# Other places for the steps of a spectral slot, and the spectrum's sum in PSUM

## Chip, cores and metric

One core of a Trainium2 chip runs the program. The metric is the device time of one execution in microseconds, as the median of several runs.

## What is computed

```python
X = np.fft.rfft(x, axis=1)                      # x: 8 x 3008 x 256
Yr = Xr @ w_r - Xi @ w_i + b_r
Yi = Xr @ w_i + Xi @ w_r + b_i
Yr, Yi = [np.sign(Y) * np.maximum(np.abs(Y) - 0.01, 0) for Y in (Yr, Yi)]
y = np.fft.irfft(Yr + 1j * Yi, n=3008, axis=1)
t = y.reshape(24064, 256)
g = t @ w_gate                                  # 256 x 1536
out = (g / (1 + np.exp(-g)) * (t @ w_val)) @ w_out
```

## The kernel before

The program has two parts: a **spectral part** (Fourier transform, mixing, shrinking, inverse transform), some 600 us long, and the feed-forward part (FFN), which takes the rest. In the FFN every product is cut into 2 x 2 blocks that take seven block products in place of eight (a Strassen scheme), and an operand is a pair of tiles, a rounded upper part and the rest (`hi`, `lo`), so that a product is three matmuls. The spectral part ends in DRAM (`xt_d`), and the FFN reads its tokens from there.

The spectral part is a pipeline of 96 **slots** (8 batches x 12). `transform` does not issue a step at once: `put(t, step)` records it with a time in slots, and `go` sorts all records by that time and issues them. So the numbers set the order on each engine, and each engine works through its own queue in that order and waits on semaphores. The steps of slot s are, with TensorE as PE, VectorE as DVE, ScalarE as ACT, GpSimd as POOL and the DMA queue as SP:

- `load_a` (L360, SP) and `b_mm` (L365, PE): 4 fp32 matmuls, the second stage of the transform, into bank `ps_b`.
- `f_steps` (L378): `im` (ACT) copies the imaginary part out of PSUM, `hi` (ACT) rounds the bank to `f_hi`; on DVE, `both` (L388) adds the real and imaginary part into the tile `f`, `hi_sum` (L394) rounds that sum, `lo_sum` (L397) takes its rest, `lo` (L400) takes the rest of the bank.
- `sum_mm` (L404, PE): six matmuls of the rounded sum and its rest into half a bank, `ps_s`. `add_bias` (L411, DVE) adds the bias and writes the result into a `mixb` bank; `mix_mm` (L417, PE) adds twelve more matmuls onto it.
- `y_steps` (L433): `turn` (ACT, four copies, L439), `clip` (DVE, L443), `shrink` (POOL, L446), `upper` (ACT, `y_hi`, L452), `lower` (DVE, `y_lo`, L455).
- `bi_mm` (L459, PE), `z_out` (L470, ACT), `z_store` (L475, SP), three to four slots later.

Between these stand **items**, none to four in a slot: `a_mm` (L344), the first stage of the transform for later batches, and `ai_mm` (L490), the last stage of the inverse. Each is followed by a copy on ACT (`a_out`, L350; `ai_out`, L496) and a store. `GAPS` gives an item's place in its slot, `AFTER` that of its copy. `A_FAST`, `A_SLOW`, `Z_AT`, `Z_SLOW` and `Z_FAST` say in which slots the items fall.

Eighteen **weight units** run beside that (L264): a load, eight DVE steps that turn float64 weights into float32 (L280 to L287), four sums on POOL (`sums`, L291), a rounding on ACT (`upper`, L303), a subtraction on POOL (`lower`, L308), a store. At the end `open_ring` (L620) frees space for a ring of four buffers, `load_unit` (L624) fills it, and the FFN's first products (L670) are issued among the last steps of the spectral part by `run` (L912).

Of the kernel before, what the change touches and what calls it, by code (L numbers as in the profile page):

```python
# [9 lines left out]
F32 = mybir.dt.float32  # L10
# [3 lines left out]
ALU = mybir.AluOpType  # L14
# [15 lines left out]
T = 512  # L30
# [6 lines left out]
HIDDEN = [P, 6, T]  # L37

KEPT = 6
A_FAST, A_KNEE, A_SLOW = 2.0, 36, 1.35  # L40
FIRST_X = {2: -0.93, 3: -0.90, 4: -0.5}
W_FIRST, W_STEP = 2, 4.2
A_SUM = False
WARM = 5
LAG, LAST = 4, 2.2
PAD = 216
Z_AT, Z_SLOW, Z_KNEE, Z_FAST = 18, 2.8, 19, 1.1
NG, GT, GW = 13, 5 * N1, 6 * N1
NU = 7
WO = 12 * GW + 4 * N1  # L50
GAPS = {1: (0.38,), 2: (0.38, 0.78), 3: (0.38, 0.78, 0.90), 4: (0.38, 0.40, 0.78, 0.90), 5: (0.36, 0.38, 0.40, 0.78, 0.90)}
AFTER = {0.36: 0.62, 0.38: 0.63, 0.40: 0.64, 0.78: 1.03, 0.90: 1.15}


A_AT = {1: 0, 2: 1, 4: 2, 5: 3, 6: 4, 7: 5, 3: 6}
# [127 lines left out]
def transform(ctx, tc, front, last, tail, ffn, ps_, xp, w_r, w_i, cb, wup_raw, wdn_raw, ca, cf, ci, co, wdn, w21, wup_d, xt_d, d2):  # L183
# [24 lines left out]
    def put(t, fn, *args):  # L208
        ops.append((t, len(ops), fn, args))
# [12 lines left out]
    d1, st = {}, {}  # L222
# [41 lines left out]
    def weight_unit(i, at):  # L264
        kind, u = ("up", i) if i < 2 * NQ else ("down", i - 2 * NQ)
        src = wup_raw[u] if kind == "up" else wdn_raw[u]
        e = scratch[:, 2 * T : 3 * T].bitcast(I32)
        w = scratch[:, : 2 * T].rearrange("p (a b) -> p a b", b=P)
        a = w[:, 0:4, :].rearrange("p a b -> p (a b)")
        m = w[:, 4:8, :].rearrange("p a b -> p (a b)")  # L270
        box = {}
        high = lambda: box["raw"][:, :, 1]
        low = lambda: box["raw"][:, :, 0]

        def load():
# [13 lines left out]
        a21, a11, a12, a22, s1, s2, s3, s4 = [w[:, j, :] for j in range(8)]  # L289

        def sums():  # L291
            g.tensor_tensor(s1, a21, a22, op=ALU.add)
            g.tensor_tensor(s2, s1, a11, op=ALU.subtract)
            g.tensor_tensor(s3, a11, a21, op=ALU.subtract)
            g.tensor_tensor(s4, a12, s2, op=ALU.subtract)

        def upper():
            if kind == "up":
                box["both"] = sb.tile([P, 2, 7, P], F32R, name="both", tag="both", bufs=1)
                box["hi"], box["lo"] = box["both"][:, 0], box["both"][:, 1]  # L300
            else:
                box["hi"], box["lo"] = [part[:, u] for part in wdn]
            act.copy(box["hi"], w[:, 1:8, :])  # L303
            if i == 3 * NQ - 1:
                act.copy(w21[:, 0, :], a21)

        def lower():
            g.tensor_tensor(box["lo"], w[:, 1:8, :], f32(box["hi"]), op=ALU.subtract)  # L308
            if i == 3 * NQ - 1:
                g.tensor_tensor(w21[:, 1, :], a21, f32(w21[:, 0, :]), op=ALU.subtract)  # L310

        def store():
            if kind == "up":
                nc.sync.dma_start(wup_d[u], f32(box["both"].rearrange("p i n a -> p i (n a)")))

        put(at - 1.5, load)
        for step, t in zip(steps, (0.39, 0.93, 0.96, 1.39, 1.93, 1.96, 2.39, 2.93)):
            put(at + t, step)
        put(at + 3.36, sums)
        put(at + 3.72, upper)  # L320
        put(at + 4.36, lower)
        put(at + 4.8, store)


    def load_first():
# [49 lines left out]
    def f_steps(b, p):  # L375
        box = {}

        def im():  # L378
            box["bank"] = st.pop(("b", b, p)).rearrange("p (a q b) -> p q a b", q=2, b=64)
            f = sb.tile([P, 2, C], F32, name="f", tag="f", bufs=2)  # L380
            box["im"], box["both"] = f[:, 0, :], f[:, 1, :]
            box["hi"] = sb.tile([P, 3, 2, P], F32R, name="f_hi", tag="f_hi", bufs=2)
            box["lo"] = sb.tile([P, 3, 2, P], F32R, name="f_lo", tag="f_lo", bufs=2)
            st["f", b, p] = box["hi"], box["lo"]
            act.copy(split(box["im"]), box["bank"][:, 1:2])

# [45 lines left out]
    def y_steps(b, p):  # L432
# [175 lines left out]
class FFN:  # L608
# [51 lines left out]
    def run(self, go, one):  # L660
# [347 lines left out]
```

## Time and profile before

| | us |
|---|---|
| median of 3 runs (2651.88 to 2654.41) | 2652.49 |
| the profiled execution's own time | 2655.08 |
| its span, first to last instruction | 2653.0 |
| spectral part, from the first sums on (38 to 598 us of the span) | 560.0 |
| FFN after it (598 to 2653) | 2055.0 |
| PE busy over the span | 2618.5 (99%) |
| DVE, ACT, POOL busy | 2079.8, 1739.5, 1919.7 |

PE counts as busy while any matmul is in flight, and a matmul's end is modelled. A short wait between two products can so hide in the busy time, and the share of 99% says little: the starts of the matmuls say more. The profiled execution took 2.6 us more than the median.

### The profile page before, as it was taken

Reading aid. Unit: us, or ns where it says so; the run is one execution under the profiler, and the core shown is the slowest. Engines: PE = TensorE matmul, PEld = TensorE weight load, DVE = VectorE, ACT = ScalarE, POOL = GpSimd, SP = SyncE. Lnnn points to the kernel's source line nnn. Section 1 sums busy time; section 2 is a strip of 40 time slices with the busy share of each in tenths; the row PEclk is TensorE's granted clock in tenths of the full one; section 3 lists DMA queues with packets and bytes.
Section 4 is the critical chain, followed back from the end, with each engine's and each line's share of the span. In section 5 each row is a group of like instructions: output and inputs, shape, how many; then the busy total and the mean of one; then the engine's idle time right before and its main releaser. Section 6 shows DMA issues by size and latency. Waiting matters only on the chain.

```text
span 2653.0 us, 39572 instructions
## 1 busy us (share of the span) xinstructions
PE 2618.5 (99%) x12984; PEld 2190.5 (83%) x12984; DVE 2079.8 (78%) x3101; ACT 1739.5 (66%) x3356; POOL 1919.7 (72%) x1459
## 2 busy tenths in 40 slices
PE   8999999999999999999999999999999999999999
PEld 5787878897888888888888888888888888888899
DVE  4888888666877787778777787878778887888787
ACT  5787877686666666666666666566666666666665
POOL 1343343247888888888888888888888888888886
PEclk8999999999999999999999999999999999999999
DMA  9999987884544554445544554454444444444453
GB/s 270 304 300 300 299 274 244 261 274 143 168 159 156 172 176 157 163 156 174 166 160 152 177 170 160 157 175 160 145 141 167 157 146 144 163 157 154 153 174 126
DMA packets 191033, 494.71 MB, mean 186 GB/s; under 512 B 17989, under 2 KB 99317, under 8 KB 190709
## 3 DMA queue, kind: packets, MB, share of 16 engines
q1 hardware_dynamic: 190829, 492.18, 56.9%
q8 instruction: 104, 1.70, 0.3%
q14 instruction: 100, 0.82, 0.1%
HBM read 381.49 MB, written 110.62 MB: 185 GB/s over the span
## 4 chain that ended last, share of the span: by engine, by line
PE 91%; DVE 4%; ACT 2%; DMA 2%; issue 1%; POOL 0%; SPq 0%; DVEq 0%; ACTq 0%; POOLq 0%
PE bank L670 76%; PE mixb L423 3%; PE ps_a L348 2%; PE ps_b L370 2%; PE ps_x L156 2%; PE ps_s L409 2%; PE ps_z L468 2%; DVE f_hi L394 1%; PE bank L156 1%; ACT t L439 1%; DMA d<-a 1%; DVE f L388 1%; DVE scratch L283 0%; DMA xt_d<-xt 0%; ACT f_hi L391 0%
## 5 line engine op out<-in xcount | busy, mean ns | idle before, releaser
L670 PE MATMUL bank<-x_parts,wup 128*128 128x512 f32 (+1 forms) x6048 | 1511.0, 385 | 0.3 <-DVE bank L805 0.2
L670 PEld LDWEIGHTS bank<-x_parts,wup 128*128 128x128 f32 x6048 | 1127.9, 188 | 221.8 <-DVE bank L805 2.8
L690 POOL TENSOR_TENSOR h_parts<-more,h_parts 128x512 fp32r<-128x512 f32 (+1 forms) x572 | 847.5, 1494 | 109.6 <-ACT h_parts L686 108.9
L690 POOL TENSOR_TENSOR h_parts<-hidden,h_parts 128x512 fp32r<-128x512 f32 (+1 forms) x431 | 562.4, 1315 | 208.0 <-ACT h_parts L686 187.8
L670 PE MATMUL bank<-h_parts,wdn_hi 128*128 128x512 f32 (+1 forms) x2014 | 612.2, 385 | 0.0
L686 ACT CAST h_parts<-hidden 128x512 fp32r<-128x512 f32 (+1 forms) x433 | 265.6, 614 | 454.7 <-DVE hidden L778 454.7
L778 DVE TENSOR_TENSOR hidden<-hidden,bank 128x512 f32<-128x512 f32 (+1 forms) x576 | 375.9, 674 | 78.2 <-PE bank L670 69.5
L670 PEld LDWEIGHTS bank<-h_parts,wdn_hi 128*128 128x128 f32 x2014 | 377.0, 188 | 72.0 <-POOL h_parts L690 0.5
L711 DVE TENSOR_TENSOR sums<-sums,bank 128x512 f32<-128x512 f32 (+1 forms) x357 | 240.3, 673 | 250.0 <-PE bank L670 249.9
L446 POOL TENSOR_TENSOR t<-t,y 128x512 f32<-128x512 f32 x96 | 122.5, 1276 | 385.8 <-DVE y L443 365.7
L670 PE MATMUL bank<-h_parts,wdn_lo 128*128 128x512 f32 (+1 forms) x1007 | 390.1, 387 | 0.0
L686 ACT CAST h_parts<-more 128x512 fp32r<-128x512 f32 (+1 forms) x572 | 349.7, 611 | 35.1 <-DVE more L681 24.3
L776 ACT ACTIVATE hidden<-bank 128x512 f32<-128x512 f32 (+1 forms) x432 | 252.6, 585 | 120.0 <-PE bank L670 115.6
L681 DVE TENSOR_TENSOR more<-hidden 128x512 f32<-128x512 f32 (+1 forms) x286 | 289.7, 1051 | 0.0
L681 DVE TENSOR_TENSOR more<-hidden,more 128x512 f32<-128x512 f32 (+1 forms) x286 | 256.5, 897 | 0.0
L783 ACT COPY bank<-bank 128x512 f32<-128x512 f32 (+1 forms) x288 | 161.6, 561 | 110.8 <-DVE hidden L778 103.7
L805 DVE TENSOR_TENSOR bank<-hidden,bank 128x512 f32<-128x512 f32 (+1 forms) x288 | 197.0, 684 | 39.2 <-PE bank L670 23.9
L658 POOL TENSOR_TENSOR x_parts<-xf,x_parts 128x512 fp32r<-128x512 f32 (+1 forms) x168 | 210.8, 1273 | 18.7 <-ACT x_parts L657 14.6
L670 PEld LDWEIGHTS bank<-h_parts,wdn_lo 128*128 128x128 f32 x1007 | 189.0, 188 | 35.1 <-DVE sums L711 0.2
L791 ACT COPY hidden<-bank 128x512 f32<-128x512 f32 (+1 forms) x288 | 167.6, 582 | 2.9 <-PE bank L670 0.5
L439 ACT COPY t<-mixb 64x256 f32<-64x256 f32 x384 | 141.0, 367 | 19.7 <-PE mixb L423 15.8
L828 DVE TENSOR_TENSOR hidden<-hidden,bank 128x512 f32<-128x512 f32 (+1 forms) x144 | 97.4, 676 | 43.7 <-PE bank L670 42.7
(104 smaller groups left out, 3055.2 us busy)
## 6 DMA issues: line engine op xcount, KB each, us to landing
wup<-wup_d SPq DMA_DIRECT2D x288, 896.0 KB
d<-a SPq DMA_DIRECT2D x128, 192.0 KB
a_in<-d SPq DMA_DIRECT2D x96, 256.0 KB
d<-z SPq DMA_DIRECT2D x96, 256.0 KB
out<-o SPq DMA_DIRECT2D x88, 256.0 KB
scratch<-xp SPq DMA_DIRECT2D x116, 192.0 KB
xt_d<-xt SPq DMA_DIRECT2D x36, 470.0 KB
xf<-xt_d SPq DMA_DIRECT2D x15, 1024.0 KB
```

The costliest lines, as they stand in the source:

```text
L439: act.copy(t[64 * half : 64 * half + 64, k * C : (k + 1) * C], mixed[p % 2][64 * k : 64 * k + 64, half * C : (half + 1) * C])
L658: self.tc.nc.gpsimd.tensor_tensor(part[:, 1, :h], src, f32(part[:, 0, :h]), op=ALU.subtract)
L670: nc.tensor.matmul(o, lhsT=weights[w], rhs=parts[x], start=start and i == 0, stop=stop and i == 2, skip_group_check=True)
L681: v.tensor_tensor(at(o, h), at(a, h), at(b, h), op=ALU.subtract)
L686: act.copy(pair[i][:, 0, :h], at(i, h))
L690: eng.tensor_tensor(pair[i][:, 1, :h], at(i, h), f32(pair[i][:, 0, :h]), op=ALU.subtract)
L711: v.tensor_tensor(o, o, spare[:, :h], op=ALU.add)
L776: act.activation(at(i, h), src, AF.Silu)
L778: v.tensor_tensor(at(i, h), at(i, h), src, op=ALU.mult)
L783: act.copy(b3[:, :h], b1[:, :h])
L791: act.copy(m5, b2[:, :h])
L805: v.tensor_tensor(b2[:, :h], m5, b3[:, :h], op=ALU.add)
```

## The change

The tables of places get other numbers, every step's; many steps had their places written at the call and now take them from tables at the head. The spectrum's sum (`both`) is written into the free half of the bank `ps_s` (in the diff `SUM_PSUM`) in place of the tile `f`; that bank is so taken at `both`, no longer at `sum_mm`. `SHRINK` and `A_SUM` are off: `shrink` stays on POOL. The work itself is the same, instruction for instruction.

```diff
-A_FAST, A_KNEE, A_SLOW = 2.0, 36, 1.35
-W_FIRST, W_STEP = 2, 4.2
-Z_AT, Z_SLOW, Z_KNEE, Z_FAST = 18, 2.8, 19, 1.1
-GAPS = {1: (0.38,), 2: (0.38, 0.78), 3: (0.38, 0.78, 0.90), 4: (0.38, 0.40, 0.78, 0.90), 5: (0.36, 0.38, 0.40, 0.78, 0.90)}
-AFTER = {0.36: 0.62, 0.38: 0.63, 0.40: 0.64, 0.78: 1.03, 0.90: 1.15}
+A_FAST, A_KNEE, A_SLOW = 2.0, 36, 1.378
+Z_AT, Z_SLOW, Z_KNEE, Z_FAST = 19.318, 2.802, 19, 1.013
+W_FIRST, W_STEP, W_LOAD = 2, 4.249, 1.492
+W_AT = (0.188, 0.8711, 1.2132, 1.4363, 1.8494, 1.8495, 2.2706, 2.9687)
+W_LATE = (2.971, 3.565, 3.797, 4.6)
+SUM_PSUM, SHRINK, A_SUM = True, False, False
+B_AT = 0.381
+F_AT = (0.394, 0.511, 0.443, 0.604, 0.625, 0.699)
+S_AT = (1.074, 1.184, 1.443)
+Y_AT = (1.003, 1.045, 1.046, 1.785, 1.888)
+I_AT = (-0.074, 0.086, 0.813)
+AHEAD = (1.796, 1.84, 1.768)
+STORE = (0.313, 0.176)
+X_AT = (85.19, 2.457, 86.085, 1.851)
+GO_FIRST, GO = 0.225, (0.082, 0.896, 1.085, 1.221, 1.555, 2.104)
+GAPS = {1: (0.399,), 2: (0.399, 0.4923), 3: (0.399, 0.4923, 0.9754), 4: (0.399, 0.4272, 0.4923, 0.9754), 5: (-0.2439, 0.399, 0.4272, 0.4923, 0.9754)}
+AFTER = {-0.2439: -0.021, 0.399: 0.449, 0.4272: 0.899, 0.4923: 1.056, 0.9754: 1.057}
...
-        for step, t in zip(steps, (0.39, 0.93, 0.96, 1.39, 1.93, 1.96, 2.39, 2.93)):
-        put(at + 3.36, sums)
-        put(at + 3.72, upper)
-        put(at + 4.36, lower)
+        for step, t in zip(steps, W_AT):
+        put(at + W_LATE[0], sums)
+        put(at + W_LATE[1], upper)
+        put(at + W_LATE[2], lower)
...
         def both():
+            st["s", b, p] = ps_.tile([P, T], F32, name="ps_s")
+            box["both"] = st["s", b, p][:, C:] if SUM_PSUM else box["sum"]
             v.tensor_tensor(split(box["both"]), box["bank"][:, 0:1], split(box["im"]), op=ALU.add)
...
-        put(s + 0.23, b_mm, b, p)
-        for fn, t in zip(f_steps(b, p), (0.40, 0.60, 0.41, 0.66, 0.71, 0.78)):
-        put(s + 1.0, sum_mm, b, p)
-        put(s + 1.26, add_bias, b, p)
-        put(s + 1.53, mix_mm, b, p)
-        for fn, t in zip(y_steps(b, p), (0.80, 1.05, 1.13, 1.54, 1.90)):
-        put(s + LAG + 0.12, bi_mm, b, p)
-        put(s + LAG + 0.26, z_out, b, p)
-        put(s + LAG + 0.45, z_store, b, p)
```

On PE, two neighbouring slots of the early spectral part, from the last products of one `mix_mm` (`mixb_135`) to the first of the next (`mixb_134`); `ps_s` is `sum_mm`, `ps_z` is `bi_mm`, `ps_b` is `b_mm`, `ps_a` is an item. Before:

```order
L423 MATMUL mixb_135<-wm_lo,f_hi 128x256
L348 MATMUL ps_a<-scratch,wa 96x512
L409 MATMUL ps_s<-wm_hi,f_hi 128x256 x2
L409 MATMUL ps_s<-wm_lo,f_hi 128x256 x2
L409 MATMUL ps_s<-wm_hi,f_lo 128x256 x2
L468 MATMUL ps_z<-y_hi,wi_hi 128x512
L468 MATMUL ps_z<-y_hi,wi_lo 128x512
L468 MATMUL ps_z<-y_lo,wi_hi 128x512
L370 MATMUL ps_b<-wf,a_in 128x128 x4
L348 MATMUL ps_a<-scratch,wa 96x512
L423 MATMUL mixb_134<-wm_hi,f_hi 128x256
```

and now:

```order
L437 MATMUL mixb_135<-wm_lo,f_hi 128x256
L360 MATMUL ps_a<-scratch,wa 96x512
L482 MATMUL ps_z<-y_hi,wi_hi 128x512
L482 MATMUL ps_z<-y_hi,wi_lo 128x512
L482 MATMUL ps_z<-y_lo,wi_hi 128x512
L423 MATMUL ps_s<-wm_hi,f_hi 128x256 x2
L423 MATMUL ps_s<-wm_lo,f_hi 128x256 x2
L423 MATMUL ps_s<-wm_hi,f_lo 128x256 x2
L382 MATMUL ps_b<-wf,a_in 128x128 x4
L360 MATMUL ps_a<-scratch,wa 96x512
L437 MATMUL mixb_134<-wm_hi,f_hi 128x256
```

The three matmuls of `bi_mm` moved from behind `sum_mm` to ahead of it.

On ACT, the slot in which a weight unit is rounded (`both` is here the weights' tile, `a` the copy of an item, `t` is `turn`). Before:

```order
L391 CAST f_hi<-ps_b 128x512
L452 CAST y_hi<-t 128x512
L353 COPY a<-ps_a 96x512
L303 CAST both<-scratch 128x896
L439 COPY t<-mixb_135 64x256 x4
```

and now:

```order
L405 CAST f_hi<-ps_b 128x512
L365 COPY a<-ps_a 96x512
L315 CAST both<-scratch 128x896
L466 CAST y_hi<-t 128x512
L453 COPY t<-mixb_135 64x256 x4
```

`y_hi` went behind the item's copy and behind the weights' rounding. POOL's subtraction of the unit (L308, now L320), which waits for that rounding, was placed behind the next slot's `shrink` and is now placed ahead of it.

On SP, where the FFN's weights are first loaded (`wup`; `d` is a `z_store`, `a_in` a `load_a`, `xt_d` an item's store). Before:

```order
L628 DMA wup<-wup_d_82 128x1792
L362 DMA a_in<-d_4687 128x2x256
L476 DMA d_7_81<-z 128x2x256
L628 DMA wup<-wup_d_88 128x1792
L476 DMA d_7_81<-z 128x2x256
L628 DMA wup<-wup_d_83 128x1792
L628 DMA wup<-wup_d_89 128x1792
L639 DMA xf<-xt_d_66 128x2x1024
L476 DMA d_7_81<-z 128x2x256 x3
```

and now:

```order
L642 DMA wup<-wup_d_82 128x1792
L642 DMA wup<-wup_d_89 128x1792
L642 DMA wup<-wup_d_88 128x1792
L516 DMA xt_d_71<-xt 256x1x188
L490 DMA d_7_81<-z 128x2x256
L642 DMA wup<-wup_d_83 128x1792
L490 DMA d_7_81<-z 128x2x256 x2
L653 DMA xf<-xt_d_66 128x2x1024
```

The loads moved behind the last `load_a`, three of them stand together, and the fourth unit (89) is ahead of the second (88). With the other `Z_` numbers the last items fall in slot 94 instead of slot 91: four slots had no item at all, now one has none.

## Rows read from the trace of the kernel before

**Rows 1.** Busy us in the slots: PE, PEld, DVE, ACT, POOL; clock, DMA share, GB/s.

```profile
38.00:598.00 560.00, 540.73 (x3630) 459.87 (x3631) 448.31 (x814) 436.38 (x977) 207.93 (x197) 0.99 0.90 281
```

**Rows 2.** Waits, 38 to 598 us: total us, times, longest.

```profile
PEld mixb L423 <- DVE mixb L414: 12.1, 23, 1.1
PE ps_s L409 <- DVE f_hi L394: 11.4, 22, 1.5
...
DVE mixb L414 <- PE ps_s L409: 4.7, 10, 0.7
...
PEld ps_x L156 <- ACT xt L498: 4.2, 3, 2.3
...
PEld ps_a L348 <- ACT a L353: 3.7, 10, 0.7
```

**Rows 3.** Timeline of PE: one slot with two items and no wait.

```profile
559.65 0.49 PE L409 MATMUL ps_s<-wm_hi,f_hi 128*128 128x256 f32 x2
...
560.46 0.39 PE L468 MATMUL ps_z<-y_hi,wi_hi 128*128 128x512 f32 x1
...
561.15 1.05 PE L370 MATMUL ps_b<-wf,a_in 128*128 128x128 f32 x8
562.04 1.13 PE L156 MATMUL ps_x<-wo,z_in 120*128 120x141 f32 x8
562.91 0.37 PE L423 MATMUL mixb<-wm_hi,f_hi 128*128 128x256 f32 x1
...
564.43 1.13 PE L156 MATMUL ps_x<-wo,z_in 120*128 120x141 f32 x8
565.30 0.50 PE L409 MATMUL ps_s<-wm_hi,f_hi 128*128 128x256 f32 x2
```

**Rows 4.** The chain of waits: an item of the first stage (start, us).

```profile
165.65 0.91 PE ps_a L348 x2
```

**Rows 5.** Lines L394 and L388 on DVE: ns min/median/max; busy us, mean ns, idle before.

```profile
L394 DVE CAST f_hi<-f x96: 293/295/1740, 37.7 to 593.6; 128x256 fp32r<-128x256 f32 x96
```

```profile
L388 DVE TENSOR_TENSOR f<-ps_b,f 128x256 f32<-128x256 f32 x95 | 39.8, 419 | 63.3 <-ACT f_hi L391 59.0 <-PE ps_x L156 4.4
```

**Rows 6.** Timeline, 239 to 246 us: a weight unit's subtraction and what follows.

```profile
239.94 2.28 POOL L308 TENSOR_TENSOR both<-scratch,both 128x896 fp32r<-128x896 f32 x1
...
240.72 1.65 DVE L394 CAST f_hi<-f 128x256 fp32r<-128x256 f32 x1
...
242.52 0.48 PE L409 MATMUL ps_s<-wm_hi,f_hi 128*128 128x256 f32 x2 [0.68 <-DVE f_hi L394]
...
245.08 0.69 DVE L414 TENSOR_TENSOR mixb<-ps_s,bias 128x512 f32<-128x512 f32 x1
...
245.82 0.19 PEld L423 LDWEIGHTS mixb<-wm_hi,f_hi 128*128 128x128 f32 x1 [0.76 <-DVE mixb L414]
```

**Rows 7.** Timeline at 559 us: `turn`, a subtraction on POOL, and `y_lo`.

```profile
558.97 1.50 ACT L439 COPY t<-mixb 64x256 f32<-64x256 f32 x4
559.08 1.28 POOL L658 TENSOR_TENSOR x_parts<-xf,x_parts 128x512 fp32r<-128x512 f32 x1 [1.17 <-ACT x_parts L657]
559.21 1.70 DVE L455 TENSOR_TENSOR y_lo<-t,y_hi 128x512 fp32r<-128x512 f32 x1
```

**Rows 8.** Line L308 on POOL and lines L452, L455: ns min/median/max.

```profile
L308 POOL TENSOR_TENSOR both<-scratch,both x12: 2102/2272/2297, 69.3 to 338.5; 128x896 fp32r<-128x896 f32 x12
```

```profile
L452 ACT CAST y_hi<-t x96: 610/624/662, 47.6 to 604.1; 128x512 fp32r<-128x512 f32 x96
```

```profile
L455 DVE TENSOR_TENSOR y_lo<-t,y_hi x96: 674/681/1700, 49.5 to 604.7; 128x512 fp32r<-128x512 f32 x96
```

**Rows 9.** Timeline of PE, slots without items: the last of four such waits.

```profile
592.81 0.36 PE L423 MATMUL mixb<-wm_hi,f_hi 128*128 128x256 f32 x1 [0.59 <-DVE mixb L414]
```

**Rows 10.** Timeline of SP: a lone load of weights; the stretch in which it moves.

```profile
604.42 0.33 SPq L628 DMA_DIRECT2D wup<-wup_d  x1
```

```profile
605.40:608.60 3.20, 2.04 (x9) 1.42 (x8) 0.01 (x1) 2.04 (x4) 0.00 (x0) 1.00 0.91 325
```

More of the change, by code (lines that the diff above doesn't have):

```diff
@@ L39 @@
 KEPT = 6
-A_FAST, A_KNEE, A_SLOW = 2.0, 36, 1.35
-FIRST_X = {2: -0.93, 3: -0.90, 4: -0.5}
-W_FIRST, W_STEP = 2, 4.2
[L43 to L46, printed above, removed]
-Z_AT, Z_SLOW, Z_KNEE, Z_FAST = 18, 2.8, 19, 1.1
+A_FAST, A_KNEE, A_SLOW = 2.0, 36, 1.378
+Z_AT, Z_SLOW, Z_KNEE, Z_FAST = 19.318, 2.802, 19, 1.013
 NG, GT, GW = 13, 5 * N1, 6 * N1
@@ L50 @@
 WO = 12 * GW + 4 * N1
-GAPS = {1: (0.38,), 2: (0.38, 0.78), 3: (0.38, 0.78, 0.90), 4: (0.38, 0.40, 0.78, 0.90), 5: (0.36, 0.38, 0.40, 0.78, 0.90)}
-AFTER = {0.36: 0.62, 0.38: 0.63, 0.40: 0.64, 0.78: 1.03, 0.90: 1.15}
+FIRST_X = {2: -0.93, 3: -0.9, 4: -0.5}
+W_FIRST, W_STEP, W_LOAD = 2, 4.249, 1.492
+W_AT = (0.188, 0.8711, 1.2132, 1.4363, 1.8494, 1.8495, 2.2706, 2.9687)
+W_LATE = (2.971, 3.565, 3.797, 4.6)
+SUM_PSUM, SHRINK, A_SUM = True, False, False
+WARM = 5
+LAG = 4
+PAD = 216
+B_AT = 0.381
[9 more added lines that the diff above has]
+AFTER = {-0.2439: -0.021, 0.399: 0.449, 0.4272: 0.899, 0.4923: 1.056, 0.9754: 1.057}
 A_AT = {1: 0, 2: 1, 4: 2, 5: 3, 6: 4, 7: 5, 3: 6}
@@ L314, in store @@
                 nc.sync.dma_start(wup_d[u], f32(box["both"].rearrange("p i n a -> p i (n a)")))
-        put(at - 1.5, load)
-        for step, t in zip(steps, (0.39, 0.93, 0.96, 1.39, 1.93, 1.96, 2.39, 2.93)):
+        put(at - W_LOAD, load)
+        for step, t in zip(steps, W_AT):
             put(at + t, step)
-        put(at + 3.36, sums)
-        put(at + 3.72, upper)
-        put(at + 4.36, lower)
-        put(at + 4.8, store)
+        put(at + W_LATE[0], sums)
+        put(at + W_LATE[1], upper)
+        put(at + W_LATE[2], lower)
+        put(at + W_LATE[3], store)
     def load_first():
@@ L380, in im @@
             f = sb.tile([P, 2, C], F32, name="f", tag="f", bufs=2)
-            box["im"], box["both"] = f[:, 0, :], f[:, 1, :]
+            box["im"], box["sum"] = f[:, 0, :], f[:, 1, :]
             box["hi"] = sb.tile([P, 3, 2, P], F32R, name="f_hi", tag="f_hi", bufs=2)
@@ L404, in sum_mm @@
     def sum_mm(b, p):
-        ps = st["s", b, p] = ps_.tile([P, T], F32, name="ps_s")
+        ps = st["s", b, p]
         n = 0
@@ L445, in shrink @@
         def shrink():
-            g.tensor_tensor(box["t"], box["t"], box["y"], op=ALU.subtract)
+            (v if SHRINK else g).tensor_tensor(box["t"], box["t"], box["y"], op=ALU.subtract)
         def upper():
@@ L506, in transform @@
         b, p = divmod(s, NP)
-        put((-0.95, -0.94, -0.89)[s] if s < 3 else s - 1.6, load_a, b, p)
-        put(s + 0.23, b_mm, b, p)
-        for fn, t in zip(f_steps(b, p), (0.40, 0.60, 0.41, 0.66, 0.71, 0.78)):
+        put((-0.95, -0.94, -0.89)[s] if s < 3 else s - AHEAD[0], load_a, b, p)
+        put(s + B_AT, b_mm, b, p)
+        for fn, t in zip(f_steps(b, p), F_AT):
             put(s + t, fn)
-        put(s + 1.0, sum_mm, b, p)
-        put(s + 1.26, add_bias, b, p)
-        put(s + 1.53, mix_mm, b, p)
-        for fn, t in zip(y_steps(b, p), (0.80, 1.05, 1.13, 1.54, 1.90)):
+        put(s + S_AT[0], sum_mm, b, p)
+        put(s + S_AT[1], add_bias, b, p)
+        put(s + S_AT[2], mix_mm, b, p)
+        for fn, t in zip(y_steps(b, p), Y_AT):
             put(s + 1 + t, fn)
-        put(s + LAG + 0.12, bi_mm, b, p)
-        put(s + LAG + 0.26, z_out, b, p)
-        put(s + LAG + 0.45, z_store, b, p)
+        put(s + LAG + I_AT[0], bi_mm, b, p)
+        put(s + LAG + I_AT[1], z_out, b, p)
+        put(s + LAG + I_AT[2], z_store, b, p)
     A_ALL, Z_ALL = (B - 1) * NCH, KEPT * NU
@@ L537, in transform @@
                 b, ch = k // NCH + 1, k % NCH
-                put(FIRST_X.get(k, t - 2.0), load_x, b, ch)
+                put(FIRST_X.get(k, t - AHEAD[1]), load_x, b, ch)
                 put(t, a_mm, b, ch, ("a", "x0", "x1")[k % 3] if s < 17 else "s" if A_SUM and gap < 0.5 else "a")
                 put(s + AFTER[gap], a_out, b, ch, "a")
-                put(s + AFTER[gap] + 0.13, a_store, b, ch)
+                put(s + AFTER[gap] + STORE[0], a_store, b, ch)
             else:
@@ L545, in transform @@
                 if cc == 0:
-                    put(t - 2.0, load_z, b, u)
+                    put(t - AHEAD[2], load_z, b, u)
                 put(t, ai_mm, b, u, cc)
@@ L549, in transform @@
                 if cc == 1:
-                    put(s + AFTER[gap] + 0.11, ai_store, b, u)
+                    put(s + AFTER[gap] + STORE[1], ai_store, b, u)
     for i in range(3 * NQ):
@@ L566, in transform @@
     for i, sums in enumerate(ffn.SUMS):
-        put(84.37 + 2 * i, ffn.x_sum, 0, *sums)
+        put(X_AT[0] + X_AT[1] * i, ffn.x_sum, 0, *sums)
     for i, n_ in enumerate(ffn.X_AT):
-        put(85.68 + 1.5 * i, ffn.x_part, 0, n_)
+        put(X_AT[2] + X_AT[3] * i, ffn.x_part, 0, n_)
     warm = k1p.tile([P, T], F32, name="warm", tag="bias")
@@ L911, in open_rest @@
             pool["sums"] = self.sb.tile([P, 3, T], F32, name="sums", bufs=1)
-        go(S + 0.2)
-        for n, after, until in ((0, 1, 0.76), (0, 5, 0.9), (0, 6, 1.0), (0, 2, 1.2), (0, 7, 1.5), (0, 3, LAST)):
+        go(S + GO_FIRST)
+        for n, after, until in zip((0,) * 6, (1, 5, 6, 2, 7, 3), GO):
             later(0, 0, n, after, lambda until=until: go(S + until))
```

## Prediction

> **What bounds the kernel now.** I read the busy time by stretches first, then the starts of the matmuls, then the waits, then the collisions that cause them. The change leaves the FFN's work and order alone but for its first steps, so only the 560 us of the slots, and the seam to the FFN, can give or cost anything. There PE is busy for 540.7 us of 560 [rows 1], with DVE at 448.3. PE's own work is less than that, since waits hide in the modelled ends. One slot in which nothing waits shows the price of each step by the starts of its matmuls [rows 3]: `sum_mm` 0.81 us, `bi_mm` 0.69, `b_mm` 0.89, an item 0.87, `mix_mm` 1.52, an item 0.87, together 5.65. The fixed steps are 3.91 us a slot, over 96 slots 375. Items after 38 us: some 108 of the first stage at 0.91 [rows 4] make 98, the 84 of the last stage (72 at 0.87 and 12 of half that) 68. That is 541 us if the slot of [rows 3] is free of waits, and 522 if a tenth of a microsecond in each `sum_mm` and `mix_mm` is a hidden wait (an estimate). So **20 to 40 us of the 560 are waits of PE**, and this is all that a new order can win.
>
> Who makes PE wait [rows 2]: `mix_mm` for `add_bias` 12.1 us in 23 waits, `sum_mm` for `hi_sum` 11.4 in 22, the last stage's items for a copy on ACT 4.2, the first stage's for theirs 3.7. Two thirds is DVE being late. Why it is late shows in one weight unit [rows 6]: POOL's subtraction runs from 239.94 for 2.28 us, and the 128x256 cast `hi_sum`, begun in the middle of it, takes 1.65 us and ends with it, where it takes 0.295 us at the median [rows 5]. `sum_mm` then waits 0.68 us, and since all of DVE's queue is now late, `mix_mm` waits 0.76 us more for `add_bias` three microseconds later. Eighteen units do this.
>
> **The change, part by part.** The sum is made against the profiled execution's 2655.1 us, which is 2.6 us above the median of the runs shown; I subtract that at the end.
>
> *The sum in PSUM.* `hi_sum` now reads PSUM, as does `lo_sum`. Its lower bound is the 0.293 us of today's shortest, its upper bound the 0.419 us of the addition `both`, which reads 128x256 from the other PSUM bank [rows 5]; I take 0.42, the row that has a PSUM input. In the other 78 slots `hi_sum` is so 0.13 us slower. Nothing shows this cast from PSUM beside a POOL instruction, but `both`, which has one input in PSUM, stays at 0.419 us in the mean of 95 [rows 5]: I take it that the collision is gone. The bank is tracked as a whole, so `sum_mm` now waits once, for `lo_sum`, not first for `hi_sum`: 0.42 us later. Against these 0.55 us stands `bi_mm`, which moved ahead of `sum_mm` and gives 0.69 us of PE work as cover. So a slot gains 0.14 us of slack where nothing collides, and loses the whole collision where it did. Of the 11.4 us I take **-10**; the ends are -11.4 and 0.
>
> [...]
>
> *The weight units, half a slot earlier.* On ACT the unit's rounding now stands right ahead of `y_hi`. POOL's subtraction starts when the rounding ends, `y_hi` takes 0.62 us beside it, and `y_lo`, which has two SBUF inputs, comes in the middle of 2.27 us [rows 8]. That such a `y_lo` blocks is shown: 1.70 us beside a POOL subtraction, against 0.68 [rows 7, 8]. So `y_lo` ends 2.27 + 0.68 = 2.95 us after the rounding, 1.5 later than alone. Behind it on DVE stand `clip`, `add_bias` and, through it, PE's `mix_mm`. But `clip` waits for `turn` anyway, which ends 0.62 + 1.50 [rows 7] = 2.12 us after the rounding, or 2.7 with an item's copy between. Left uncovered are 0.25 to 0.83 us in 18 units: 4.5 to 15 us of late `mix_mm`, against today's 12.1, most of which comes from the collision that goes. I take **+2**; the ends are -8 (4.5 less 12.1) and +15 (18 x 0.83, nothing saved).
>
> [...]
>
> *`add_bias`.* It loses the 0.69 us of `bi_mm` between `sum_mm` and `mix_mm`. `b_mm` and one item remain, 0.89 + 0.87 = 1.76 us, for an addition of 0.69 [rows 6]. It waited for `sum_mm` itself only 4.7 us in 10 waits [rows 2]: I take 0, and price the other case below.
>
> *`y_hi` behind the item's copy.* The bank of the first-stage items is free one ACT instruction (0.62 us) earlier, ahead of the item behind `mix_mm`. Of the 3.7 us I take **-3.5**; ends -3.7 and 0.
>
> *Items to the end.* Slots without items go from four to one; each cost one wait of some 0.5 us, the last 0.59 [rows 9]: **-1.5**, ends -2.4 and 0. The last-stage items come at one unit a slot, not 1.1: their copies wait less for buffers whose stores are under way. Of 4.2 us [rows 2] I take **-2**; ends -4.2 and +2.
>
> *The seam.* The FFN's first weights are loaded only when the last item and the `z_out` behind it are done. After issue a load takes 1.0 us to start and 3.2 to move [rows 10]. From the end of that last `bi_mm` PE has a sum, a `b_mm`, a `mix_mm`, a `bi_mm`, a sum, 4.7 us, some 5.2 with a wait; ACT has `turn` (1.50 [rows 7]), a short copy and `z_out` (a copy like `y_hi`, 0.62 at most), some 2.4 us, before SP can issue: 2.4 + 4.2 = 6.6. I take **+2**. Ends: 0, and +8 if the two loads issued behind it share the engines evenly, 2.4 + 1.0 + 9.6 = 13.
>
> *All else* (places of loads and stores on SP, of the x parts on POOL and ACT) I cost at 0: the DMA share is 0.90 in the slots [rows 1] and the bytes are the same; if that cover goes, it is in the range's ends.
>
> Sum: -10 + 2 - 3.5 - 1.5 - 2 + 2 = **-13 us**: 2642.1 for the profiled execution, 2639.5 as a median.
>
> **The rivals.**
> - (a) *The collision only moves.* DVE's load stays: -18 x 1.23 us for `hi_sum`, +18 x 1.5 for `y_lo`, +78 x 0.13. Then `mix_mm` gets what `sum_mm` gave: +12 in place of +2, -3 in all, **2649.5**. For it: DVE's 80% in the slots. Against: `turn` runs beside the block.
> - (b) *Slower: the lost cover of `add_bias`.* Three slots of each of the 18 units hold weight steps on DVE; there DVE is late by itself, and 0.69 us less between sum and mix could show in each of these 54. It decides if DVE comes to `add_bias` later than 1.07 us after the sum's end (1.76 less 0.69). At two thirds of 0.69 us in all 54 it is +25: -13 + 25 = +12, **2664.5**; from 0.34 us a slot on, the kernel is slower by what can be told. For it: 23 waits of this kind already. Against: `add_bias` itself waits for the sum only 10 times.
> - (c) *The loads at the seam come evenly*: +8 in place of +2, **2645.5**. For it: three stand together in the queue. Against: nothing shown either way.
> - (d) *Nearly all goes*: all lower ends but that of the seam, -11.4 - 8 - 3.7 - 2.4 - 4.2 + 2 = -28, **2625**.
> - (e) *No effect*, as the slots have another bound, DMA at a share of 0.90: **2652.5**. Against: no wait of PE for a load is in [rows 2].
>
> **How the numbers follow.** Chances: forecast 0.48, (a) 0.18, (b) 0.13, (c) 0.07, (d) 0.11, (e) 0.03. The range for 8 in 10 reaches from just under (d), 2623, to just under (b), 2661. A measurement can tell 0.2%, 5.3 us, from no change. Faster than 2647.2: 0.42 of the forecast's 0.48 (its own spread is some 10 us to either side, as its terms rarely meet their ends together), 0.05 of (c), all of (d), 0.06 of (a): 0.64. Slower than 2657.8: (b) and 0.02 of (a): 0.15. Within: 0.06 of the forecast, 0.10 of (a), 0.02 of (c), (e): 0.21.
>
> **What would show it.** Right: no `hi_sum` over 0.5 us, mean near 0.42; waits of `sum_mm` on DVE under 3 us; 18 `y_lo` of some 2.2 us; waits of the first-stage items under 1 us; a PE wait of 1 to 3 us at the FFN's first product. Wrong: `mix_mm` waiting over 25 us for `add_bias`, or any new wait of PE of over 5 us in total that is named nowhere above.

## The result, and the profile after

The changed kernel takes **2627.2 us** (4 runs, 2626.9 to 2629.5), the kernel before beside it 2653.45: a ratio of 0.990, 95% interval 0.9886 to 0.992, or 26 us gained where I had forecast 13. The profiled execution (2627.16 us) is a typical one.

Nearly all of it lies ahead of the FFN, whose first product starts at 569.72 us, before at 596.06. The row is the busy time by stretch of the changed kernel from 38 us to the FFN's start (columns: stretch, its length, busy time and instructions of PE, PEld, DVE, ACT, POOL, granted clock, DMA share, GB/s). The stretch was 560 us long [rows 1], now 534:

```profile
38.00:572.00 534.00, 528.84 (x3623) 455.52 (x3623) 451.11 (x810) 439.98 (x976) 205.79 (x196) 1.00 0.90 289
```

PE idled visibly for 560.00 - 540.73 = 19.3 us before and 5.2 now: 14 us of the 26. The other 12 stood in busy time. I take most of them for waits hidden there, as a matmul's end is modelled. Some 2 us are the clock (an estimate, half of the 4.9 us between these two): the granted clock was at 0.50 of full speed for 7.7 us of this stretch before and for 2.8 us now. Of the 7.7 us, 3.4 stand right behind a wait of PE for an item's copy (the product that waited, then the stretch behind it; the last columns are granted clock, DMA share, GB/s):

```profile
485.96 2.23 PE L156 MATMUL ps_x<-wo,z_in 120*128 120x141 f32 x8 [2.07 <-ACT xt L498]
...
486.00:489.40 3.40, 3.40 (x15) 3.40 (x16) 1.69 (x5) 2.12 (x5) 0.00 (x0) 0.50 1.07 354
```

DVE and ACT are each some 3 us busier, though the collision of [rows 6] is gone: they do as much work in 26 us less.

Where along the slots the time comes from shows in the start of `im` (ACT's first step of a slot, L385 before, L397 now) in both traces:

| slot | 0 | 16 | 36 | 60 | 72 | 76 | 88 | 95 |
|---|---|---|---|---|---|---|---|---|
| before, us | 36.31 | 128.71 | 245.10 | 385.12 | 456.35 | 486.72 | 556.59 | 592.26 |
| after, us | 34.28 | 125.11 | 238.21 | 372.23 | 439.57 | 462.02 | 527.93 | 566.49 |
| lead, us | 2.0 | 3.6 | 6.9 | 12.9 | 16.8 | 24.7 | 28.7 | 25.8 |

Two gains stand out: a steady one of 13 us over slots 16 to 72, where the weight units run, and **8 us in the four slots from 72 to 76**, where my terms had 2 us. Not all of the 8 us is won. Before, eleven items stand in these slots, now eight (the last stage's items in this stretch, before and now; columns PE, PEld and ACT, where ACT's copies count the items; before, one first-stage item comes on top):

```profile
456.35:486.72 30.37, 10.81 (x75) 9.68 (x74) 4.99 (x10) 0.99 0.75 223
...
439.57:462.02 22.45, 7.94 (x58) 7.24 (x57) 4.00 (x8) 1.00 0.71 222
```

Three items, some 2.6 us, are only put off, so some 5 us are won. By slot 92 the changed kernel is six items behind. It makes them up in slots 92 to 94, where the kernel before has none, and so some 3 us of the lead go back at the end.

The waits of the changed kernel, slots only, by PE and PEld (columns: engine, the line that waits, who ended the wait, us in total, times, longest). Line numbers are 12 to 14 higher than before: L360 is `a_mm`, L423 `sum_mm`, L437 `mix_mm`, L428 `add_bias`, L411 `lo_sum`.

```profile
PE ps_a L360 <- DMA scratch<-xp: 1.9, 1, 1.9
PE ps_s L423 <- DVE f_lo L411: 1.2, 4, 0.3
PE mixb L437 <- DVE mixb L428: 1.1, 2, 0.6
...
PEld mixb L437 <- DVE mixb L428: 11.4, 22, 1.5
PEld ps_s L423 <- PE ps_z L482: 6.0, 16, 0.7
```

`sum_mm`'s 11.4 us for DVE [rows 2] are 1.2 now, and the waits for the items' copies are off the list. The 1.2 us are four waits of 0.29 to 0.31 us of its first product, which reads `f_hi` alone and yet waits for `lo_sum`, as I had said of the bank. `mix_mm`'s waits for `add_bias` are as long as before: 12.5 us with those of PE and PEld added, against 13.4 before (the 12.1 of [rows 2] and 1.3 us of PE's own).

The forms of three DVE steps (columns: line, engine, operation, tiles, count: shortest/median/longest in ns, first and last start, shape), and of POOL's subtraction:

```profile
L408 DVE CAST f_hi<-ps_s x96: 423/424/425, 35.6 to 567.9; 128x256 fp32r<-128x256 f32 x96
...
L469 DVE TENSOR_TENSOR y_lo<-t,y_hi x96: 679/683/2186, 48.2 to 578.2; 128x512 fp32r<-128x512 f32 x96
...
L295 DVE SCALAR_TENSOR_TENSOR scratch<-raw,scratch x18: 691/693/694, 50.9 to 456.8; 128x512 int32<-128x512 int32 x18
...
L320 POOL TENSOR_TENSOR both<-scratch,both x12: 2099/2111/2122, 63.3 to 325.1; 128x896 fp32r<-128x896 f32 x12
```

No `hi_sum` is long any more. Eighteen `y_lo` take 1.9 to 2.2 us, one in each weight unit, as I had said. One of these units in order of time (columns: start, duration, engine, line, operation, tiles, shape; in brackets the idle time before it and what ended it), ACT and POOL first, then DVE and PE:

```profile
228.65 0.94 ACT L315 CAST both<-scratch 128x896 fp32r<-128x896 f32 x1
229.49 0.62 ACT L466 CAST y_hi<-t 128x512 fp32r<-128x512 f32 x1
230.01 1.50 ACT L453 COPY t<-mixb 64x256 f32<-64x256 f32 x4
...
227.78 1.30 POOL L460 TENSOR_TENSOR t<-t,y 128x512 f32<-128x512 f32 x1
229.66 2.10 POOL L320 TENSOR_TENSOR both<-scratch,both 128x896 fp32r<-128x896 f32 x1 [0.58 <-ACT both L315]
...
230.15 2.17 DVE L469 TENSOR_TENSOR y_lo<-t,y_hi 128x512 fp32r<-128x512 f32 x1
232.24 0.41 DVE L457 TENSOR_SCALAR y<-t 128x512 f32<-128x512 f32 x1
232.58 0.69 DVE L428 TENSOR_TENSOR mixb<-ps_s,bias 128x512 f32<-128x512 f32 x1
...
233.32 0.39 PE L437 MATMUL mixb<-wm_hi,f_hi 128*128 128x256 f32 x1 [0.62 <-DVE mixb L428]
```

`y_lo` begins inside POOL's subtraction and ends 0.56 us behind it (232.32 against 231.76). `turn` runs until 231.51, so some 0.8 us of the block are uncovered for `clip`, `add_bias` and `mix_mm`, which waits 0.62 us.

At the seam (SP's queue and PE): the FFN's loads are issued 0.03 us after the last item's product ends, and PE reaches the FFN at 569.72 without waiting.

```profile
563.55 0.58 PE L168 MATMUL ps_x<-wo,z_in 96*128 96x94 f32 x4
...
564.16 1.34 SPq L642 DMA_DIRECT2D wup<-wup_d  x3
...
569.72 0.50 PE L934 MATMUL bank<-x_parts,wdn_hi 128*128 128x512 f32 x1
570.05 0.84 PE L684 MATMUL bank<-x_parts,wup 128*128 128x512 f32 x3
```

### The profile page after: what moved, and what is told of

Its sections match the earlier page's. It is cut to its first block, busy times and chain, and to the rows that moved or that the text cites. A ratio compares the mean times of both kernels' runs of the same rounds, so it can differ in the third digit from the quotient of the medians.

```text
span 2625.3 us, 39519 instructions
## 1 busy us (share of the span) xinstructions
PE 2605.8 (99%) x12984; PEld 2186.7 (83%) x12984; DVE 2084.4 (79%) x3101; ACT 1743.3 (66%) x3356; POOL 1918.7 (73%) x1459
## 4 chain that ended last, share of the span: by engine, by line
PE 96%; DVE 1%; DMA 1%; ACT 1%; issue 0%; POOL 0%; SPq 0%; DVEq 0%; ACTq 0%; POOLq 0%
PE bank L684 77%; PE mixb L437 5%; PE ps_a L360 4%; PE ps_b L382 3%; PE ps_x L168 3%; PE ps_s L423 2%; PE ps_z L482 2%; PE bank L168 1%; DMA d<-a 1%; DMA d<-z 0%; DMA a_in<-d 0%; DVE y_lo L469 0%; PE ps_z L479 0%; PE mixb L590 0%; DVE ps_s L402 0%
## 5 line engine op out<-in xcount | busy, mean ns | idle before, releaser
L672 POOL TENSOR_TENSOR x_parts<-xf,x_parts 128x512 fp32r<-128x512 f32 (+1 forms) x168 | 211.1, 1275 | 20.1 <-ACT x_parts L671 17.4
```

The costliest lines, as they stand in the source:

```text
L672: self.tc.nc.gpsimd.tensor_tensor(part[:, 1, :h], src, f32(part[:, 0, :h]), op=ALU.subtract)
```

## The experiments

**Gain** below is the time against the kernel before, run beside it, and **lost** is 26.3 less that gain. Each gain's interval is some 4 us to either side, so a lost figure is known to some 6 us. Every edit is one to the tables of places, so one part is taken back while the rest stays, or put alone into the old order. A part that is taken back meets the others at their new places: the run shows what it is worth there, not what it gave on the way from the kernel before.

A trace shows one execution, and one thing differs between them that no edit aims at. In most traces PE waits near 96 us for one load of an input chunk, and in or behind this wait the granted clock falls to 0.50 in six of them. This is the trace of the run with POOL's subtraction moved, below: the item that waited, `mix_mm` at the lower clock, `mix_mm` at the full one, and the stretch at 0.50.

```profile
99.54 2.02 PE L360 MATMUL ps_a<-scratch,wa 96*96 96x512 f32 x2 [4.06 <-DMA scratch<-xp]
...
102.00 0.41 PE L437 MATMUL mixb<-wm_hi,f_hi 128*128 128x256 f32 x1
102.21 0.41 PE L437 MATMUL mixb<-wm_hi,f_lo 128*128 128x256 f32 x1
...
109.01 0.27 PE L437 MATMUL mixb<-wm_hi,f_lo 128*128 128x256 f32 x1
109.13 0.28 PE L437 MATMUL mixb<-wm_lo,f_hi 128*128 128x256 f32 x1
...
98.30:105.10 6.80, 5.56 (x17) 3.91 (x17) 2.64 (x7) 3.81 (x9) 0.00 (x0) 0.50 1.01 374
```

The matmuls start 0.21 us apart in place of 0.12, so 6.8 us at 0.50 cost PE some 3 us (an estimate) on top of the wait. The changed kernel's own trace has a wait of 1.9 us there and no such stretch behind it.

**The sum back in SBUF, all places new.**

```diff
-SUM_PSUM, SHRINK, A_SUM = True, False, False
+SUM_PSUM, SHRINK, A_SUM = False, False, False
```

> All places of the change, but the spectrum's sum back in SBUF, so that hi_sum again has an SBUF source. Theory S (the PSUM source is what ends the collision, as my first term says): a part of the 18 hi_sum of the slots with a weight unit is long again (over 0.5 us), sum_mm waits 8 to 11 us for it, 2635 to 2638 us. Theory P (the new places end it: in the changed kernel's trace the long subtraction starts at 206.28, 1.6 us behind the start of hi_sum at 204.64): hi_sum stays near 0.3 us but for a tenth or two where a 0.46 us POOL addition runs, sum_mm waits under 3 us, 2624 to 2630 us.

2631.8 us against 2651.8: gain 20.0 (ratio 0.992, 0.991 to 0.994), **lost 6.3**. Between the two theories. The collision is back, though: 16 `hi_sum` over 0.4 us, and 9 long ones of `lo_sum`, which now has two SBUF inputs:

```profile
L408 DVE CAST f_hi<-f x96: 293/294/1399, 36.3 to 570.9; 128x256 fp32r<-128x256 f32 x96
...
L411 DVE TENSOR_TENSOR f_lo<-f,f_hi x96: 424/426/2218, 36.6 to 571.6; 128x256 fp32r<-128x256 f32 x96
```

`sum_mm` waits for DVE only 3.5 us in all, so the new order covers most of what the old one let through. In this trace `im` is 3.0 us behind the changed kernel's in slot 95, and all of that comes between slots 20 and 24: one collision makes PE wait 1.4 us for `lo_sum`, and behind it the granted clock is at 0.50 for 3.4 us (159.3 to 162.7).

**The sum in PSUM alone, all places old** (the change's `SUM_PSUM = True`, every table as before).

> All places of before, only the sum in PSUM. The collision of hi_sum with the 2.27 us subtraction must go here if a PSUM source goes past it, no hi_sum over 0.5 us. Theory S (this is 10 us of the 26): 2641 to 2645 us. Theory P (the old order has no cover ahead of sum_mm, which now waits for lo_sum, 0.55 us later in each of the 78 other slots): the gain is eaten, 2648 to 2660 us.

2649.9 against 2651.8: gain 1.9, no difference that can be told (0.9984 to 1.0003). Here all 96 `hi_sum` take 424 to 426 ns, and little is won: over the slots (38 to 592 us) `sum_mm` waits 10.7 us for `lo_sum` in 19 waits, in place of the 11.4 us for `hi_sum` in 22. In this trace slots 8 to 12 take 3.4 us longer than in the kernel before; PE waits 2.3 us for an item's copy there, and the granted clock is at 0.50 for 6.8 us (99.1 to 105.9). So ending the collision is worth little by itself here, and how little is known to some 3 us.

**`bi_mm` back behind the sum product**, and **the sum in PSUM and `bi_mm` ahead, in the old order** (the first two numbers of `I_AT` new, all other places old).

```diff
-I_AT = (-0.074, 0.086, 0.813)
+I_AT = (0.12, 0.26, 0.813)
```

> The changed kernel with bi_mm and z_out back behind the sum product. Theory C (bi_mm's 0.69 us is what covers the later sum_mm): sum_mm waits for lo_sum in most slots, some 0.3 us in 60 of them, and only part comes back as cover of add_bias: 2634 to 2645 us. Rival (the cover is as good behind the sum, where add_bias uses it): 2624 to 2629 us, with the waits of mix_mm for add_bias gone instead.

> The kernel before with only the sum in PSUM and bi_mm ahead of the sum product, the two parts on which my first term of -10 us rests. Theory C: no long hi_sum, sum_mm's waits on DVE under 4 us, 2640 to 2644 us. Rival (the places of all DVE and ACT steps and of the weight units are needed too, since what sum_mm no longer waits for mix_mm now does): 2646 to 2652 us, with more than 15 us of waits of mix_mm for add_bias.

The first: 2638.8 against 2653.3, gain 14.6, **lost 11.7** (0.993 to 0.996). The second: 2642.3 against 2653.3, **gain 11.0** (0.994 to 0.997). The times are those of Theory C in both. With `bi_mm` behind, `sum_mm` waits 6.4 us for `lo_sum`, in 18 waits and not in the 60 that I had expected, and the sum's weight load waits behind `mix_mm` 50 times, where it waited 16 times behind `bi_mm`:

```profile
PEld ps_s L423 <- PE mixb L437: 21.9, 50, 0.9
...
PEld mixb L437 <- DVE mixb L428: 6.9, 19, 1.1
```

The waits for `add_bias` do fall, from 12.5 to 7.1 us, as the rival said; this cover is worth less than the other. PSUM gives 1.9, PSUM and `bi_mm` together 11.0. I read the two as one step: the cover makes room for the later start that PSUM costs. But no run has `bi_mm` ahead alone in the old order, so how the 11.0 splits is open; that the sum in SBUF cost only 6.3 with all places new speaks for a large share of `bi_mm`.

**The weight units at their old places**, whole and the late part alone (POOL's additions, the rounding, the subtraction, the store).

```diff
-W_FIRST, W_STEP, W_LOAD = 2, 4.249, 1.492
-W_AT = (0.188, 0.8711, 1.2132, 1.4363, 1.8494, 1.8495, 2.2706, 2.9687)
-W_LATE = (2.971, 3.565, 3.797, 4.6)
+W_FIRST, W_STEP, W_LOAD = 2, 4.2, 1.5
+W_AT = (0.39, 0.93, 0.96, 1.39, 1.93, 1.96, 2.39, 2.93)
+W_LATE = (3.36, 3.72, 4.36, 4.8)
```

> The changed kernel with the weight units' steps and loads back at their old places (sum in PSUM). The subtraction then meets hi_sum, which reads PSUM, and y_lo is free. If the block of y_lo (18 of some 2.1 us, 11.4 us of waits of mix_mm for add_bias) is what the new places cost: 2617 to 2623 us, and those waits under 5 us. If the new places of the units are themselves a part of the gain: 2630 to 2640 us, with the waits in another place.

> The changed kernel with only the late part of a weight unit (POOL's additions, ACT's rounding, POOL's subtraction, the store) back at its old places; the eight DVE steps stay new. All the late part back with the DVE steps cost 8.4 us. If the gain is in the late part (the rounding and the subtraction half a slot earlier, which I had priced at +2): 2632 to 2637 us. If it is in the eight DVE steps (whose L295 takes 0.69 us at its new place and 1.39 at the old one, 18 times): 2624 to 2629 us.

2635.6 against 2651.8 (gain 16.2, **lost 10.1**; 0.992 to 0.995) and 2634.5 against 2653.4 (gain 19.0, **lost 7.3**; 0.992 to 0.995). (The 8.4 us in the second expectation is the plain difference of the two medians; against the kernel beside it, it is 10.1.) So in the new order the new places of the units are needed, and most of that is the late part, the piece that I had priced at a loss. In the second run (the waits of ACT, then of DVE):

```profile
ACT both L315 <- POOL scratch L307: 16.0, 12, 1.9
...
ACT wdn_hi L315 <- POOL scratch L307: 6.3, 6, 1.8
...
DVE y_lo L469 <- ACT y_hi L466: 26.1, 19, 2.1
```

At the old places POOL's four additions stand behind `shrink`, so the rounding, ahead of `y_hi` in ACT's queue, waits for them in all 18 units, 22.3 us in all, and `y_hi`, `y_lo` and all of DVE behind them are late. In the changed kernel the additions stand ahead of `shrink`: of these waits 0.3 us is left, and `y_lo` waits 6.7 us for `y_hi`. The kernel before had the additions behind `shrink` too, but the rounding behind `y_hi`, so that its waits held neither `y_hi` nor `y_lo`. They were shorter there:

```profile
ACT both L303 <- POOL scratch L295: 7.0, 9, 0.9
...
ACT wdn_hi L303 <- POOL scratch L295: 1.7, 4, 0.9
```

So the two runs make an order that neither kernel has, and their loss is not what the move gave from the kernel before on; no run shows that. What the DVE steps gain themselves, 18 `L295` of 0.69 us where the old places give 1.39, is the rest at most.

**The block of `y_lo` taken away**: POOL's subtraction behind the next `shrink`.

```diff
-W_LATE = (2.971, 3.565, 3.797, 4.6)
+W_LATE = (2.971, 3.565, 4.06, 4.6)
```

> The changed kernel with only the 128x896 subtraction moved on POOL, from ahead of one shrink to behind the next one, so that it lies between a shrink and the y_lo that follows 3 us later. Theory: the 18 long y_lo go (none over 1 us), the waits of mix_mm for add_bias fall from 11.4 us to under 4, 2617 to 2622 us. Rival (turn, which runs beside the block, covers it): y_lo short all the same, the waits stay over 8 us, 2625 to 2629 us.

2627.5 against 2651.8: gain 24.3, the changed kernel's time within the interval. Five `y_lo` over 0.9 us are left, the longest 1.81; the waits for `add_bias` fall from 12.5 to 8.5 us. By the time and the waits the rival holds: the block does cost, but little. In this trace the start of `im` is 4.5 us behind the changed kernel's in slot 18 (140.56 and 136.03) and 3.3 in slot 95 (569.77 and 566.49), so some 1.2 us come from it over all units. The 4.5 us come before that, 2.7 of them between slots 8 and 12, where the rows at the head of this section stand: PE waits for the input chunk 4.1 us here and 1.9 in the changed kernel, and the clock is at 0.50 from 98.3 to 105.1. This execution was the slowest of its four (2630.55 us).

**The numbers of the items back**, and **the places of loads and stores back.**

```diff
-A_FAST, A_KNEE, A_SLOW = 2.0, 36, 1.378
-Z_AT, Z_SLOW, Z_KNEE, Z_FAST = 19.318, 2.802, 19, 1.013
+A_FAST, A_KNEE, A_SLOW = 2.0, 36, 1.35
+Z_AT, Z_SLOW, Z_KNEE, Z_FAST = 18, 2.8, 19, 1.1
```

```diff
-I_AT = (-0.074, 0.086, 0.813)
-AHEAD = (1.796, 1.84, 1.768)
-STORE = (0.313, 0.176)
+I_AT = (-0.074, 0.086, 0.45)
+AHEAD = (1.6, 2.0, 2.0)
+STORE = (0.13, 0.11)
```

(and `W_LOAD` 1.5.)

> The changed kernel with only the numbers of the items back (which slot has how many; the places within a slot stay new). In the runs so far the lead over the kernel before grows by some 9 us between slots 72 and 78, where before 3 copies into xt wait 9.3 us for stores. Theory I (the number of items per slot does this): that step goes, 2634 to 2638 us, and copies into xt wait for stores again. Rival (the places of loads and stores do it): the step stays, 2626 to 2630 us.

> The changed kernel with only the places of its loads and stores on SP back (how far ahead each load stands, where each store stands, the weights' loads). Theory I: within 2 us of the changed kernel, 2625 to 2629 us. Rival: the step at slots 72 to 78 goes here, 2634 to 2640 us.

Items: 2636.6 against 2653.3, gain 16.7, **lost 9.5** (0.992 to 0.995). The copies into `xt` (L498 before, L512 now) wait for stores again. First the kernel before from 440 to 500 us, then this run from 440 to 495; the changed kernel has no such wait in that stretch:

```profile
ACT xt L498 <- DMA xt_d<-xt: 9.3, 3, 4.3
...
PE ps_x L156 <- ACT xt L498: 3.6, 3, 2.1
```

```profile
ACT xt L512 <- DMA xt_d<-xt: 9.8, 4, 5.9
DVE ps_s L402 <- PE ps_x L168: 6.6, 2, 5.5
...
PE ps_x L168 <- ACT xt L512: 2.0, 1, 2.0
```

PE waits directly only 2 to 4 us. But the waiting copy holds ACT's queue, and behind it `im`, `hi`, `turn` and so the chain of the slots. From slot 72 to 76 this run takes 5.7 us longer than the changed kernel, of the step of 8 us; three items more, some 2.6 us, are in that.

Loads and stores: 2642.7 against 2653.3, lost 15.7, but not for the reason asked about. With these numbers the load of chunk 5 of the second batch comes ahead of that of chunk 4, which then lands on chunk 0 before its use; the run computes that batch with chunk 4 in place of chunk 0, and its first product waits 14.6 us for this load. From then on the run is constantly behind: 12.4 us in slot 12 (115.76 and 103.33), 13.5 in slot 95 (580.04 and 566.49). So the places as such cost about 1 us over 83 slots, and the gain at slot 72 stays.

**The item's copy back behind `y_hi`.**

```diff
-AFTER = {-0.2439: -0.021, 0.399: 0.449, 0.4272: 0.899, 0.4923: 1.056, 0.9754: 1.057}
+AFTER = {-0.2439: -0.021, 0.399: 0.79, 0.4272: 0.899, 0.4923: 1.056, 0.9754: 1.057}
```

> The changed kernel with the item's copy out of ps_a (the first of a slot) back behind y_hi and its store with it. My term of -3.5 us: 2630 to 2632 us, with waits of the next item for that copy of 3 us and more. Rival (the bank was no bound once the rest moved): 2625 to 2629 us, no such wait over 1 us in total.

2636.1 against 2653.4: gain 17.4, **lost 8.9** (0.992 to 0.995). Of it 5.5 us stand as waits of the next item, and 2.1 in the wait for an input chunk:

```profile
PE ps_a L360 <- ACT a L365: 5.5, 6, 1.8
PE ps_a L360 <- DMA scratch<-xp: 4.0, 1, 4.0
```

The granted clock is at 0.50 for 6.8 us behind that load and for 3.4 us (256.5 to 259.9) behind one of the waits for the copy. The four executions lie between 2632.4 and 2636.8 us, and the trace is the slowest. `y_hi` itself has moved since, so the copy stands at 0.79 of its slot here and at 0.63 in the kernel before. The loss shows that the copy's place matters in the new order; its size holds more than that.

**Two tries to beat it**: `clip` and `shrink` behind `add_bias`; the same with POOL's subtraction behind that `shrink` (`W_LATE[2] = 4.21`).

```diff
-Y_AT = (1.003, 1.045, 1.046, 1.785, 1.888)
+Y_AT = (1.003, 1.2, 1.201, 1.785, 1.888)
```

> The changed kernel with clip and shrink behind add_bias instead of ahead of it. In its trace every late add_bias (42 in which mix_mm starts with the addition's end) comes right behind a clip, which waits for turn on ACT. Theory (this queue is what keeps the 12.5 us of waits of mix_mm for add_bias): they fall under 6 us, 2617 to 2623 us. Rival (the long y_lo ahead of both is what is late, and a later shrink delays y_hi): 2626 to 2634 us.

> As the run before, and POOL's long subtraction behind that shrink, so that y_lo is free too. Theory (block and queue hide one another, only both together free add_bias): waits of mix_mm for add_bias under 3 us, 2612 to 2620 us. Rival (bi_mm then waits for the later y_hi, or a slot is bound by PE's own work): 2624 to 2632 us.

2628.5 (gain 24.9) and 2633.7 (gain 19.8) against 2653.4: not faster than the change, and the second some 6.5 us slower. In the first the waits of PEld for `add_bias` fall from 11.4 to 7.2 us, but 4.6 us for `clip` come in, and `shrink` now lies on a step of the weight unit, 18 times:

```profile
L295 DVE SCALAR_TENSOR_TENSOR scratch<-raw,scratch x18: 1632/1660/1668, 51.0 to 458.0; 128x512 int32<-128x512 int32 x18
```

0.69 us became 1.66. In the second, 3.8 of the 6.5 us come between slots 8 and 12, where PE waits 5.2 us for the input chunk and the clock is at 0.50 for 6.8 us. No kernel here is faster than the changed one.

## Why the prediction was right, and which sizes were not

The direction and most of the signs held: no `hi_sum` over 0.43 us, waits of `sum_mm` on DVE 1.2 us, 18 long `y_lo`, first-stage items that no longer wait for their copy. The wait of PE at the FFN's first product did not come. The time lies in the range, but near rival (d), which had a chance of 0.11, and the forecast of 13 us is half of the 26. Point by point ("taken back" is what was lost when only that part went back to its old place):

| step of the prediction | I took, us | the runs |
|---|---|---|
| sum in PSUM, `bi_mm` as its cover | -10 | -11.0 alone in the old order; taken back 6.3 and 11.7 |
| weight units half a slot earlier | **+2** | taken back **10.1, of it 7.3 the late part**; from the kernel before on: not shown |
| `add_bias` without `bi_mm` | 0 | its waits 12.5 us, 13.4 before |
| the item's copy ahead of `y_hi` | -3.5 | taken back 8.9, of it 5.5 waits |
| items to the end, stores | -1.5 - 2 | taken back **9.5** |
| the seam | +2 | 0 |
| loads and stores on SP | 0 | about 1 |

- *The first term* is right in size, and in mechanism as far as the runs go: PSUM ends the collision (no `hi_sum` over 0.426 us with all places old), and without `bi_mm` as cover it gives nothing that can be told (1.9 us). How much `bi_mm` gives without PSUM is open.
- *The weight units* were priced by the wrong piece. I followed the new block of `y_lo`, which came as described (2.17 us in the rows above, 0.8 uncovered) and costs some 1 us, and missed what stood in the same order: POOL's additions move ahead of `shrink`, and ACT no longer waits for them. With the rounding now ahead of `y_hi`, that is worth 7.3 us. The lower end of -8 was argued from other waits.
- *The copy and the items* are mis-sized. Both terms were taken from waits of PE: 3.7 and 4.2 us [rows 2]. PE's share of a late ACT queue is only what is left after its covers; copies into `xt` alone waited 9.3 us for stores, and all of ACT stood behind them.
- *The seam*: I had SP wait for `z_out` behind the last item. By the trace it waits for the item's product alone, so the 2.4 us of ACT's work that I put in between do not count.
- *Rival (a)*, the collision only moves, did happen in DVE's rows and cost some 1 us: `turn` covers it. Its three terms for DVE's load do not cancel, as the prediction has it: -22 + 27 + 10 is +15 us. Measured, DVE is busy 2.8 us more. *Rival (b)* falls: `add_bias` waits for the sum 16.0 us, not 4.7, yet `mix_mm` no longer than before. *Rival (e)* falls with the DMA share at 0.90 as before, in less time.

The losses add up to more than the gain: 6.3 + 11.7 + 10.1 + 8.9 + 9.5 = 46.5 us for 26.3. The parts are not independent; a slot that is late for one reason has time for another. That the time lies in the range is in part luck: each of the large terms behind the first was too small, and the range was wide enough to hold it.

Open: why PE waits 0.6 to 5.2 us near 96 us for one load of an input chunk, in kernels that leave its place alone; in the changed kernel it is the longest wait of PE that is left. What it and the lower clock behind it add to a lost figure, up to some 4 us by the traces, need not be the edit's. And whether `shrink` on L295 is all that undoes the last two tries: no run took it away there.

## What to carry to other kernels

Price a moved step by everything that stands in its queues, not by the waits of the bound engine: a 9 us wait of a copy on ACT showed as 4 us on PE, and taking the part back cost 9.5. When an order changes on several engines, look in each queue for what is no longer waited for, as well as for what is newly blocked. A value moved to PSUM to dodge a collision paid here only together with other work in front of its reader, which starts later: 1.9 us alone, 11.0 with `bi_mm` ahead. Before reading a lead slot by slot, count what was put off; before reading a loss from a part taken back, ask whether the mixed order makes a wait that neither kernel had.

## What was not expected of the hardware

- `lo_sum` is as exposed as `hi_sum`: with both inputs in SBUF it took up to 2.218 us (the run with the sum back in SBUF, median 0.426), with one in PSUM 0.423 to 0.426 in the changed kernel. I read this as the block that `y_lo` shows in the rows above: begun 0.49 us into POOL's subtraction of 2.10 us, it took 2.17 us against 0.68. A weight step did the same: L295 (L283 before) took 1.39 us in the kernel before, begun at 245.68 beside a `shrink` that runs from 245.24 for 1.28 us, and 1.66 in the run with `clip` and `shrink` moved, against 0.69 in the changed kernel.
- The cast from PSUM takes 0.424 us, as long as the subtraction of that shape, and a little more than the 0.419 us that I had as its upper bound. From SBUF it takes 0.294 at the median (the run with the sum back in SBUF).
- The granted clock fell to 0.50 in the middle of the slots, in or behind waits of PE: for 3.4 us behind a wait of 2.07 us in the kernel before, for 6.8 us at waits of 3.1 to 5.2 us for the input chunk in four runs. It did not behind 1.9 us in the changed kernel, nor behind 3.0 us for the input chunk in the run with `clip` and `shrink` alone moved.
